# Four more half tasks of a convolution on GpSimd, paired in four phases, in a fused convolution and feed-forward kernel

## The chip, the cores and the metric

The kernel runs on one core of a Trainium2 chip. The metric is the device time of one execution in microseconds. Five engines work beside each other: TensorE (PE, with its weight loads as PEld), VectorE (DVE), ScalarE (ACT), GpSimd (POOL), and SyncE (SP), which here only issues DMAs.

## The reference

A lightweight convolution over 8 sequences of 3904 rows and 192 columns comes first: 8 heads of 24 columns, each with its own 7 causal taps (a softmax of `weight`). Its result goes through a multiplicative feed-forward network without nonlinearity.

```python
w = exp(weight - max);  w = w / (sum(w) + 1e-9)          # 8 heads x 7 taps
out[b, s, h, g] = sum_k w[h, k] * x_pad[b, s + k, h, g]   # 6 rows of zeros ahead of each sequence
x = out.reshape(31232, 192)
a = x @ w1; b = x @ w2                                    # 192 -> 1024, twice
h = a * b @ w3                                            # 1024 -> 1024
return h @ w_out                                          # 1024 -> 192
```

## The kernel before

**Tiling.** The 31232 rows are two streams (r = 0, 1) of 15616, which lie side by side on the partitions: 64 columns of each stream make 128 partitions, so 192 columns are k = 0, 1, 2. A stream is cut into rounds R = 0 to 30 of 512 rows. `first_product(R)` makes x @ w1 (pa) and x @ w2 (pb) for 8 blocks ft of 128 of the 1024 columns, each pa and pb in a pair of PSUM banks from a ring of four pairs (`banks`). ACT copies pa to `asb` (L603), DVE multiplies it with pb into `abT` (L605). `second_product(R, r)` multiplies abT with w3 @ w_out, computed once at the start, into `ops` (L621); ACT copies it to `osb` (L626) and SP sends it out.

**Phases.** Three rounds make a phase p. In its first stage the first products of its rounds run, in its second stage the second products, numbered n = 0 to 5. The order on every engine is the order in which the code issues; it is written out by hand. The first products of phase 0 run ahead of the loop, phases 1 to 8 have three rounds in both stages, phases 9 and 10 finish.

**The convolution** is done in three ways. A pair of rounds is called q: rounds 2q+1 and 2q+2.
- On TensorE: batches b of 26-row windows (`conv`, L328): x is loaded by GpSimd DMAs (`x_jobs`, L158) into `xb` tiles, a banded matrix `Aband` per head is multiplied with it, ACT copies the result to `convo` (L337). `store` (SP) writes it to the DRAM tensor `rows`, and `transposes` (SP, L426) reads it back transposed into `xT`. Batches 4, 5 and 6 (rounds 5 to 8, 13 to 16, 21 to 24) are split into units of two heads, 32 matmuls each, and `places` says after which second products of which phase a unit stands (`convolve`).
- On DVE: for the pairs in `SIDE`, `side_cast` (GpSimd DMA, L480) converts 64 columns of x to bf16 in the DRAM tensor `rows_c`, `side_transpose` (SP, L489) brings it into a `raw` tile, ACT makes the tap d = 1 (`side_first`, L494), and DVE adds the other six taps (`side_sums`, L512) into a `side` tile. A planner fills second stages with these sums by their cost (`rooms`); `starts[p]` are the tasks that begin in phase p.
- On GpSimd: seven half tasks (`BY_POOL`: a pair q, a k, one of its two rounds), one per phase in phases 2 to 8, all seven taps there (`pool_sums`): per tap a product with one tensor (L539) and an add (L559; the last, L554, writes the side tile).

`operand` gives the first product its input: the side tile for pairs in `SIDE`, xT otherwise.

**GpSimd's queue.** `points` are eight places (round, ft) in a first stage. At each, GpSimd copies two elements of abT (`pace`, L876), which makes it wait for DVE, and then issues its DMAs and the parts of its half task for that point. `clear` (L860) zeroes the rows of xb ahead of a sequence.

**SP's queue** has, at the end of a first stage, xT transposes that are due (`turn`), the raw transposes of the next phase's tasks, and `pool_transpose` (L533) for the next phase's half task; then output stores and row stores as the second products come; then what is called `late`.

Of the kernel before, what the change touches and what calls it, by code (L numbers as in the profile page):

```python
# [16 lines left out]
def kernel(  # L17
# [38 lines left out]
    def phase_of(R):  # L56
        return (R - 1) // 2

    def windows(t0, t1):
# [250 lines left out]
    def conv(b, c0, wd, evict=(nc.scalar.copy,), es=None):  # L310
        n, m, E = shape_of(b)
        es = range(E) if es is None else es
        if b not in convo_of:
            convo_of[b] = work.tile([128, n, NP, NS, Q], BF16, tag="convo", bufs=2,
                                    name="convo")
            left_of[b] = D * E
        convo = convo_of[b]
        cps = {e: banks("cps") for e in es}
        c = c0
        while c < c0 + wd:  # L320
            h = c // G
            c1 = min(h * G + G, c0 + wd)
            for j in range(4):
                xb, s = xb_of[b][j]
                for e in es:
                    for r in range(NS):
                        o = cps[e][j * C:j * C + C, r, 0:m * wd]
                        nc.tensor.matmul(  # L328
                            o.rearrange("p (w g) -> p w g", g=wd)[:, :, c - c0:c1 - c0],
                            Aband[group(r, e), h, :], xb[group(r, e), s:s + m, c:c1],  # L330
                            start=True, stop=True)
            c = c1
        for f, e in zip(evict, es):
            src = cps[e][:, :, 0:m * wd].rearrange("p r (w g) -> p r w g", g=wd)
            o = 0
            for k, lo, c in segments(c0, wd):
                f(out=convo[:, e::E, k, :, lo:lo + c]  # L337
                    .rearrange("p w r g -> p r w g"), in_=src[:, :, :, o:o + c])
                o += c
        left_of[b] -= wd * len(es)  # L340
        if not left_of[b]:
            del xb_of[b]
# [27 lines left out]
    def store(b, first=0, js=range(4)):  # L370
        n = SIZES[b] // 4
        convo = convo_of[b]
        for j in js:
            w = 0
            while w < n:
                i, m = FIRST[b] + j * n + w, 1
                t, s0, s1 = wins[i]
                while w + m < n and wins[i + m] == (t + m * ST, 0, ST):
                    m += 1
                if i < first:  # L380
                    m = first - i
                elif s1 - s0 < ST:
                    m = 1
                    if s1:
                        nc.sync.dma_start(
                            out=rows[t + s0:t + s1, :],
                            in_=convo[C * j + s0:C * j + s1, w].rearrange("s k r g -> s (k r g)"))
                else:
                    src = convo[C * j:C * j + ST, w:w + m].rearrange("s w k r g -> s w (k r g)")
                    dst = rows[t:t + ST * m, :].rearrange("(w s) c -> s w c", s=ST)  # L390
# [31 lines left out]
    def transposes(R, first=0):  # L422
        t0, t1 = max(R * CH, first), min((R + 1) * CH, TS)
        a = ring_of[R] * CH % RING + t0 - R * CH
        for k in range(NP):
            nc.sync.dma_start_transpose(  # L426
                out=xT[k][:, a:a + t1 - t0], in_=rows[t0:t1, k * 128:(k + 1) * 128])
# [21 lines left out]

    BY_POOL = ((5, 2, 0), (5, 2, 1), (8, 2, 0), (8, 2, 1), (12, 2, 0), (12, 2, 1), (13, 2, 0))  # L450
    tasks = []
# [67 lines left out]

    pool_raw, pool_acc, pool_tmp = [], [], const.tile([128, CH], FP32, name="tmp")  # L520

    def pool_tiles():
        t = stage.tile([128, 3 * CH + HALO], BF16, tag="wo", bufs=1, name="acc")
        pool_acc.append(t[:, 0:2 * CH].bitcast(FP32))
        pool_raw.append(t[:, 2 * CH:3 * CH + HALO])

# [3 lines left out]

    def pool_transpose(p, k, half):
        _, _, t0, _ = pool_half(p, k, half)
        nc.sync.dma_start_transpose(out=pool_raw[0], in_=rows_c[t0 - HALO:t0 + CH, k, :])  # L533

    def pool_sums(p, k, half):
        _, _, t0, starts = pool_half(p, k, half)

        def product(out, d):
            nc.gpsimd.tensor_scalar(  # L539
                out=out, in0=pool_raw[0][:, HALO - d:HALO - d + CH],  # L540
                scalar1=wC[:, k, K - 1 - d:K - d], scalar2=None, op0=ALU.mult)

        def job(d):
            def run():
                acc, tmp = pool_acc[0], pool_tmp
                if d == 1:
                    product(acc, 1)
                    for z in starts:
                        nc.gpsimd.memset(acc[:, z - t0:z - t0 + 1], 0.0)
                    return  # L550
                product(tmp, d)
                if d == 0:
# [8 lines left out]
            return run  # L561
        return [job(d) for d in list(range(1, K)) + [0]]

    def operand(R, k, rs):
        if phase_of(R) in side_of:
# [9 lines left out]

    abT_of = {}

# [3 lines left out]
    def first_product(R, between=None):  # L581
# [4 lines left out]
        for f0 in range(0, JT, per):  # L586
# [15 lines left out]
            asb = work.tile([128, NS, CH], BF16, tag="asb", bufs=3, name="asb")  # L602
            nc.scalar.copy(out=asb[:, :, 0:per * N], in_=pa[:, :, 0:per * N])  # L603
            if per == 1:
                nc.vector.tensor_tensor(out=ab[:, f0, :, 0:N], in0=asb[:, :, 0:N],  # L605
# [169 lines left out]
    def later_loads():  # L775
# [9 lines left out]
        for i in starts[1]:  # L785
            for f in side_cast(i):
# [22 lines left out]
             for n in [max(v for v in (2, 4) if v * shape_of(b)[1] * G <= CH)]  # L809
             for h in range(0, H, n)]  # L810
    assert sum(map(len, places.values())) == len(units)
    points = ((0, 1), (0, 4), (0, 7), (1, 2), (1, 5), (2, 0), (2, 3), (2, 6))
    jobs = {p: [] for p in range(1, len(phases))}
    for p, b, part, n in ((1, 5, 0, 0), (1, 5, 1, 4), (3, 6, 0, 0), (4, 6, 1, 0)):
# [3 lines left out]
        jobs[p + 1] += todo[n:]  # L818
    pool_from = {p: v for p, v in enumerate(BY_POOL, 1)}
    pool_sum = {p + 1: pool_sums(*v) for p, v in pool_from.items()}  # L820
    casts = [(p - 1, f) for p in starts if p > 1 for i in starts[p] for f in side_cast(i)]
    casts += [(p, f) for p, (q, k, h) in pool_from.items()
              for f in side_cast(None, (q, k, *half_of(q, h)))]
    casts.sort(key=lambda c: c[0])
    for p in jobs:
        due_now = sum(d <= p for d, _ in casts)
        ahead = max(due_now, min(len(casts), len(points) - len(jobs[p])))
        now = [f for _, f in casts[:ahead]]
        jobs[p] = now + jobs[p] if p in (1, 3) else jobs[p] + now
        del casts[:ahead]  # L830
# [32 lines left out]
    for p, (rounds, ends) in enumerate(phases):  # L863
        todo = jobs.pop(p, [])

        last = len(points) - 1
        counts = [0] * 3 + [2] * 4 if p == 1 else [2] * 2 + [1] * 5
        at = [[todo.pop(0) for _ in range(min(n, len(todo)))] for n in counts + [len(todo)]]
        if p in places:
            at[last - 1].insert(0, clear)  # L870
        for v, f in enumerate(pool_sum.pop(p, ())):
            at[v].append(f)

        def issue(R, ft, fs):
            def run():
                P(out=pace, in_=abT_of[R][0:1, ft, 1, 0:2])  # L876
                for f in fs:
                    f()
            return run

        for j, R in enumerate(rounds):
            first_product(R, {ft: issue(R, ft, at[v])
                              for v, (a, ft) in enumerate(points) if a == j and at[v]})
        assert not todo
        clear()
# [8 lines left out]
        if p in pool_from:  # L894
            pool_transpose(*pool_from[p])
# [50 lines left out]
```

## Time and profile before

| | us |
|---|---|
| median of 3 runs | 510.87 (510.76 to 511.51) |
| profiled execution | 510.92 |
| its span | 509.2 |
| DVE busy in the span | 446.4 (88%) |
| ACT busy | 347.2 (68%) |
| GpSimd busy | 229.3 (45%) |

The span is from the first to the last instruction of the program; 1.7 us of the profiled execution lie around it. A busy time is the time in which at least one instruction of that engine ran. A phase T starts here with its first pa matmul; phases 1 to 8 start at 69.93, 117.07, 166.04, 213.18, 261.24, 309.35, 356.54 and 403.73 us. In rows of a timeline, the first number is the start, the second the length, and in brackets stands the idle time of the engine ahead of it with what ended it. In rows of groups, the last parts are busy time, the mean of one in ns, and the idle time ahead.

### The profile page before, as it was taken

To read this page: it belongs to the slowest core of one execution; us is meant where nothing else is said; L and a number is where in the kernel's file an instruction comes from. 1 tells how busy PE (TensorE), PEld (TensorE's weight loads), DVE (VectorE), ACT (ScalarE), POOL (GpSimd) and SP (SyncE) were. 2 spreads that over 40 slices of the span, in tenths; PEclk is the share of its full clock that TensorE was granted. 3 is DMA by queue.
4 is the path that set the end of the run, shared out by engine and by line. 5 is a ranking of instruction groups with operands and counts; after the bars stand their busy time and mean duration, and the time that the engine had idled before them with its cause. 6 is when DMAs were issued, how large, how long until landed. Compare 5 with 4: busy or idle time off the path is not lost.

```text
span 509.2 us, 13681 instructions
## 1 busy us (share of the span) xinstructions
PE 503.8 (99%) x5758; PEld 338.5 (66%) x5758; DVE 446.4 (88%) x402; ACT 347.2 (68%) x386; POOL 229.3 (45%) x303
## 2 busy tenths in 40 slices
PE   8999999999999999999999999999999999999997
PEld 4546864595569557845875596569557855965597
DVE  7898769999999799899989999999899999999930
ACT  6786667836778776477667767763776477457752
POOL 9966101333980597079519902970573067100000
PEclk9999999999999999999999999999999999999999
DMA  9999979999955999963889337975501400230024
GB/s 136 158 162 174 173 152 177 148 163 194 159 60 159 143 158 133 229 79 23 65 219 96 24 106 127 192 110 155 102 1 43 156 4 0 84 106 1 1 63 156
DMA packets 156825, 58.45 MB, mean 115 GB/s; under 512 B 112607, under 2 KB 156763, under 8 KB 156763
## 3 DMA queue, kind: packets, MB, share of 16 engines
q0 software_dynamic: 70560, 16.85, 37.2%
q1 hardware_dynamic: 86043, 40.62, 36.1%
q8 instruction: 45, 0.74, 0.6%
q14 instruction: 17, 0.14, 0.1%
q10 hardware_dynamic: 160, 0.10, 0.1%
HBM read 33.97 MB, written 34.85 MB: 135 GB/s over the span
## 4 chain that ended last, share of the span: by engine, by line
PE 98%; DMA 1%; ACT 0%; POOL 0%; DVE 0%; issue 0%; POOLq 0%
PE ops L621 32%; PE pa L596 31%; PE pb L596 31%; PE cps L328 1%; PE wps L693 1%; DMA xb<-in_x_dram 1%; PE tps L401 0%; PE ops L646 0%; PE tps L416 0%; DVE abT L605 0%; PE cps L357 0%; ACT asb L603 0%; POOL xb L158 0%; ACT convo L337 0%; ACT osb L650 0%
## 5 line engine op out<-in xcount | busy, mean ns | idle before, releaser
L605 DVE TENSOR_TENSOR abT<-asb,pb 128x1024 bf16<-128x1024 bf16 x240 | 292.7, 1221 | 30.4 <-ACT asb L603 14.5
L603 ACT CAST asb<-pa 128x1024 bf16<-128x1024 f32 x244 | 247.0, 1012 | 64.2 <-PE pa L596 64.0
L596 PEld LDWEIGHTS <-wn 64*128 64x128 bf16 x1488 | 138.5, 94 | 79.7 <-issue 1.6
L596 PEld LDWEIGHTS <-ws 64*128 64x128 bf16 x1488 | 129.7, 94 | 70.0 <-issue 1.4
L621 PE MATMUL ops<-W_sb,abT 128*128 128x192 bf16 x1936 | 163.7, 246 | 0.0
L621 PEld LDWEIGHTS <-abT 128*128 128x128 bf16 x1936 | 158.5, 98 | 6.4 <-issue 6.4
L596 PE MATMUL pb<-xT,wn 64*128 64x512 bf16 x408 | 111.2, 376 | 0.0
L596 PE MATMUL pa<-xT,wn 64*128 64x512 bf16 x408 | 110.1, 376 | 0.1
L596 PE MATMUL pa<-xT,ws 64*128 64x512 bf16 x408 | 110.1, 376 | 0.0
L596 PE MATMUL pb<-xT,ws 64*128 64x512 bf16 x408 | 108.5, 376 | 0.0
L626 ACT COPY osb<-ops 128x768 f32<-128x768 f32 (+1 forms) x61 | 48.5, 795 | 84.7 <-PE ops L621 82.3
L876 POOL COPY pace<-abT 1x2 bf16<-1x2 bf16 x57 | 10.9, 192 | 175.5 <-DVE abT L605 155.0
L596 PE MATMUL pb<-side,wn 64*128 64x512 bf16 (+1 forms) x336 | 88.8, 368 | 0.0
L596 PE MATMUL pa<-side,ws 64*128 64x512 bf16 (+1 forms) x336 | 87.3, 369 | 0.0
L596 PE MATMUL pa<-side,wn 64*128 64x512 bf16 (+1 forms) x336 | 87.3, 369 | 0.0
L512 DVE SCALAR_TENSOR_TENSOR acc<-raw,wC,acc 128x1024 f32<-128x1024 bf16 (+2 forms) x70 | 84.6, 1209 | 2.0
L596 PE MATMUL pb<-side,ws 64*128 64x512 bf16 (+1 forms) x336 | 85.7, 368 | 0.0
L539 POOL TENSOR_SCALAR tmp<-acc,wC 128x512 f32<-128x512 bf16 x42 | 65.8, 1566 | 1.2
L559 POOL TENSOR_TENSOR acc<-acc,tmp 128x512 f32<-128x512 f32 x35 | 44.4, 1267 | 2.9
L480 POOL DMA_DIRECT2D rows_c<-in_x_dram x50 | 37.1, 744 | 4.7 <-issue 2.7
L158 POOL DMA_DIRECT2D xb<-in_x_dram x50 | 32.2, 649 | 6.9 <-DMA xb<-in_x_dram 2.2
L512 DVE SCALAR_TENSOR_TENSOR acc<-side,wC,acc 128x1024 f32<-128x1024 bf16 (+1 forms) x20 | 24.3, 1217 | 3.8 <-ACT acc L494 3.2
(76 smaller groups left out, 186.9 us busy)
## 6 DMA issues: line engine op xcount, KB each, us to landing
out_dram<-osb SPq DMA_DIRECT2D x54, 384.0 KB
xb<-in_x_dram POOLq DMA_DIRECT2D x16, 240.0 KB, 7.2
out_dram<-osb SPq DMA_DIRECT2D x12, 192.0 KB
rows_c<-in_x_dram POOLq DMA_DIRECT2D x16, 130.0 KB, 5.6
rows_c<-in_x_dram POOLq DMA_DIRECT2D x12, 128.0 KB, 5.7
rows<-convo SPq DMA_DIRECT2D x6, 240.0 KB
xb<-in_x_dram POOLq DMA_DIRECT2D x6, 228.0 KB, 4.9
w3b<-in_moe_w_dram POOLq DMA_DIRECT2D x4, 256.0 KB, 5.5
```

Source lines behind the costliest of these rows:

```text
L158: nc.gpsimd.dma_start(out=tiles[js[0]][0][group(r, e), s:s + w, :], in_=bass.AP(tensor=x.tensor, offset=(r * TS + t - PAD) * D, ap=[[D, C] ...
L328: nc.tensor.matmul(o.rearrange("p (w g) -> p w g", g=wd)[:, :, c - c0:c1 - c0], Aband[group(r, e), h, :], xb[group(r, e), s:s + m, c:c1], ...
L480: nc.gpsimd.dma_start(out=rows_c[lo:t1, k, r * Q:r * Q + Q], in_=x_rows[r * TS + lo:r * TS + t1, k * Q:k * Q + Q])
L512: nc.vector.scalar_tensor_tensor(out=side_of[p][:, k, o:o + t1 - t0] if last else a, in0=raw[:, HALO + lo - t0 - d:HALO + hi - t0 - d], sc ...
L539: nc.gpsimd.tensor_scalar(out=out, in0=pool_raw[0][:, HALO - d:HALO - d + CH], scalar1=wC[:, k, K - 1 - d:K - d], scalar2=None, op0=ALU.mult)
L559: nc.gpsimd.tensor_tensor(out=a, in0=a, in1=tmp[:, lo - t0:hi - t0], op=ALU.add)
L596: nc.tensor.matmul(p[:, r, f * N:f * N + N], w_of(i, k, r)[rs, ft * 128:(ft + 1) * 128], operand(R, k, rs), start=(k == 0), stop=(k == NP ...
L603: nc.scalar.copy(out=asb[:, :, 0:per * N], in_=pa[:, :, 0:per * N])
L605: nc.vector.tensor_tensor(out=ab[:, f0, :, 0:N], in0=asb[:, :, 0:N], in1=pb[:, :, 0:N], op=ALU.mult)
L621: nc.tensor.matmul(ops[:, g // 2, (g % 2) * D:(g % 2) * D + D], ab[:, jt, r, g * 128:(g + 1) * 128], W_sb[:, jt, :], start=(jt == 0), stop ...
L626: nc.scalar.copy(out=osb.rearrange("p (a g) d -> p a (g d)", g=2), in_=ops[:, 0:ng // 2, 0:2 * D])
L876: P(out=pace, in_=abT_of[R][0:1, ft, 1, 0:2])
```

## The change

- Four half tasks more go to GpSimd: k = 0 of the pairs 10 and 11 (`PART`), two halves each. Phases 3, 4, 5 and 6 have two half tasks (lanes 0 and 1), phases 2, 7 and 8 one as before. Their results lie in a tile taken from the `xb` ring (`part_tile`).
- Batch 6 therefore starts at the third head (`first_k`): heads 0 and 1 are not computed on TensorE, k = 0 is neither stored nor transposed. Its three units stand after n = 0, 2 and 4 of phase 5; before, its four units stood after n = 2, 4 of phase 4 and n = 1, 3 of phase 5.
- GpSimd's products have two tensors: the tap is read as a tensor of 512 equal elements.
- In a phase with two lanes ACT has made the tap d = 1 of both at the end of the phase before, after n = 4 and ahead of a unit there (`pool_first`). GpSimd does the other six taps of lane 0 and then of lane 1 at point (0, 0), behind a pace copy from asb of the first block.
- All other GpSimd work of such a phase (clear, casts, loads of x) stands at the last point (2, 6), behind the sums. The raw transposes of the next phase's tasks move to the end of the phase (`late`). The casts of half tasks from phase 4 on are due a phase earlier.
- From phase 2 on the pool transposes stand ahead of the raw transposes on SP.

```diff
+    PART = {10: (0,), 11: (0,)}
+    def beside(q, k):
+        return q in SIDE or k in PART.get(q, ())
+    def first_k(b):
+        return min(k for k in range(NP) if not beside(phase_of(tok(FIRST[b] + 1) // CH), k))
...
-            left_of[b] = D * E
+            left_of[b] = (D - first_k(b) * Q // G * G) * E
...
-                f(out=convo[:, e::E, k, :, lo:lo + c]
-                    .rearrange("p w r g -> p r w g"), in_=src[:, :, :, o:o + c])
+                if k >= first_k(b):
+                    f(out=convo[:, e::E, k, :, lo:lo + c]
+                        .rearrange("p w r g -> p r w g"), in_=src[:, :, :, o:o + c])
...
-    BY_POOL = ((5, 2, 0), (5, 2, 1), (8, 2, 0), (8, 2, 1), (12, 2, 0), (12, 2, 1), (13, 2, 0))
+    POOL_AT = {2: ((5, 2, 0),), 3: ((5, 2, 1), (10, 0, 0)), 4: ((8, 2, 0), (10, 0, 1)),
+               5: ((8, 2, 1), (11, 0, 0)), 6: ((12, 2, 0), (11, 0, 1)), 7: ((12, 2, 1),),
+               8: ((13, 2, 0),)}
+    BY_POOL = [t for ts in POOL_AT.values() for t in ts]
...
+    def pool_first(lane, p, k, half):
+        nc.scalar.activation(
+            out=pool_acc[lane], in_=pool_raw[lane][:, HALO - 1:HALO - 1 + CH],
+            func=ACT.Copy, scale=wC[:, k, K - 2:K - 1])
...
-            nc.gpsimd.tensor_scalar(
-                out=out, in0=pool_raw[0][:, HALO - d:HALO - d + CH],
-                scalar1=wC[:, k, K - 1 - d:K - d], scalar2=None, op0=ALU.mult)
+                nc.gpsimd.tensor_tensor(
+                    out=acc if d == 1 else tmp, in0=pool_raw[lane][:, HALO - d:HALO - d + CH],
+                    in1=wC[:, k, K - 1 - d:K - d].to_broadcast([128, CH]), op=ALU.mult)
...
-        return [job(d) for d in list(range(1, K)) + [0]]
+        return [job(d) for d in list(range(1 if own else 2, K)) + [0]]
...
-    places = {0: (1, 2, 3, 4), 2: (0, 1, 3, 4), 4: (2, 4), 5: (1, 3)}
+    places = {0: (1, 2, 3, 4), 2: (0, 1, 3, 4), 5: (0, 2, 4)}
...
-    casts += [(p, f) for p, (q, k, h) in pool_from.items()
+    casts += [(p if p < 3 else p - 1, f) for p, v in pool_from.items() for q, k, h in v
...
-        counts = [0] * 3 + [2] * 4 if p == 1 else [2] * 2 + [1] * 5
+        lanes = pool_sum.pop(p, ())
+        counts = [0] * 7 if len(lanes) > 1 else [0] * 3 + [2] * 4 if p == 1 else [2] * 2 + [1] * 5
...
+        elif len(lanes) > 1:
+            at[last].insert(0, clear)
+        for fs in lanes:
+            for v, f in enumerate(fs):
+                at[v if len(lanes) == 1 else 0].append(f)
+        if p == 3:
+            part_tile()
...
-                P(out=pace, in_=abT_of[R][0:1, ft, 1, 0:2])
+                P(out=pace, in_=abT_of[R][0:1, ft, 1, 0:2] if ft else asb_of[0][0:1, 1, 0:2])
...
-        late = [i for i in raws if p == 0 or i >= 5 and chain[p][0][0] <= i - 5]
+        late = [i for i in raws if p == 0 or len(lanes) > 1 or i >= 5 and chain[p][0][0] <= i - 5]
+        if p > 1:
+            for lane, t in enumerate(pool_from.get(p, ())):
+                pool_transpose(lane, *t)
...
+            if n == 4 and len(pool_from.get(p, ())) > 1:
+                for lane, t in enumerate(pool_from[p]):
+                    pool_first(lane, *t)
             if n in places.get(p, ()):
                 convolve(p)
             side_steps(p, n + 1, state)
```

More of the change, by code (lines that the diff above doesn't have):

```diff
@@ L371, in store @@
         n = SIZES[b] // 4
-        convo = convo_of[b]
+        convo = convo_of[b][:, :, first_k(b):]
+        cols = slice(first_k(b) * NS * Q, NP * NS * Q)
         for j in js:
@@ L385, in store @@
                         nc.sync.dma_start(
-                            out=rows[t + s0:t + s1, :],
+                            out=rows[t + s0:t + s1, cols],
                             in_=convo[C * j + s0:C * j + s1, w].rearrange("s k r g -> s (k r g)"))
@@ L389, in store @@
                     src = convo[C * j:C * j + ST, w:w + m].rearrange("s w k r g -> s w (k r g)")
-                    dst = rows[t:t + ST * m, :].rearrange("(w s) c -> s w c", s=ST)
+                    dst = rows[t:t + ST * m, cols].rearrange("(w s) c -> s w c", s=ST)
                     for s0, s1 in ((0, 16), (16, ST)):
@@ L425, in transposes @@
         for k in range(NP):
+            if beside(phase_of(R), k):
+                continue
             nc.sync.dma_start_transpose(
@@ L520, with part_tile @@
     pool_raw, pool_acc, pool_tmp = [], [], const.tile([128, CH], FP32, name="tmp")
+    pool_more = const.tile([128, 3 * CH + HALO], BF16, name="acc")
     def pool_tiles():
-        t = stage.tile([128, 3 * CH + HALO], BF16, tag="wo", bufs=1, name="acc")
-        pool_acc.append(t[:, 0:2 * CH].bitcast(FP32))
-        pool_raw.append(t[:, 2 * CH:3 * CH + HALO])
+        for t in (stage.tile([128, 3 * CH + HALO], BF16, tag="wo", bufs=1, name="acc"), pool_more):
+            pool_acc.append(t[:, 0:2 * CH].bitcast(FP32))
+            pool_raw.append(t[:, 2 * CH:3 * CH + HALO])
+    def part_tile():
+        t = work.tile([128, XN], BF16, tag="xb", bufs=5, name="side")
+        o = 0
+        for q, ks in PART.items():
+            n = len(ks) * 2 * CH
+            side_of[q] = t[:, o:o + n].rearrange("p (k t) -> p k t", k=len(ks))
+            o += n
     def pool_half(p, k, half):
@@ L574, in w_of @@
         return (wn if k == r else wsw)[i]
-    abT_of = {}
+    abT_of, asb_of = {}, {}
     def width(R):
@@ L603, in first_product @@
             nc.scalar.copy(out=asb[:, :, 0:per * N], in_=pa[:, :, 0:per * N])
+            asb_of[0] = asb
             if per == 1:
@@ L809 @@
              for n in [max(v for v in (2, 4) if v * shape_of(b)[1] * G <= CH)]
-             for h in range(0, H, n)]
+             for h in range(first_k(b) * Q // G, H, n)]
     assert sum(map(len, places.values())) == len(units)
@@ L828 @@
         now = [f for _, f in casts[:ahead]]
-        jobs[p] = now + jobs[p] if p in (1, 3) else jobs[p] + now
+        jobs[p] = now + jobs[p] if p in (1, 3, 4) else jobs[p] + now
         del casts[:ahead]
@@ L882 @@
             first_product(R, {ft: issue(R, ft, at[v])
-                              for v, (a, ft) in enumerate(points) if a == j and at[v]})
+                              for v, (a, ft) in enumerate(((0, 0),) + points[1:] if
+                                                          len(lanes) > 1 else points)
+                              if a == j and at[v]})
         assert not todo
-        clear()
+        if len(lanes) < 2:
+            clear()
         if p == 0:
@@ L893 @@
                 side_transpose(i)
-        if p in pool_from:
-            pool_transpose(*pool_from[p])
+        if p == 1:
+            pool_transpose(0, *pool_from[p][0])
         state = set()
```

22 lines of the change are left out of this document (9 added, 13 removed).

## The prediction

> **What bounds the kernel now.** I read the page first: TensorE is busy all the time and the chain that ended last is TensorE's.
>
> ```profile
> span 509.2 us, 13681 instructions
> PE 503.8 (99%) x5758; PEld 338.5 (66%) x5758; DVE 446.4 (88%) x402; ACT 347.2 (68%) x386; POOL 229.3 (45%) x303
> PE 98%; DMA 1%; ACT 0%; POOL 0%; DVE 0%; issue 0%; POOLq 0%
> ```
>
> A busy PE is modelled, so I then cut the span into phases (p = 2 to 5 here) at the first pa matmul of each, as the chain gives them, and read the table of windows. Columns: stretch, length, busy time of each engine.
>
> ```profile
> 117.07:166.04 48.97, 48.97 (x610) 31.77 (x612) 45.99 (x37) 38.17 (x44) 28.00 (x33) 1.00 0.80 142
> 166.04:213.18 47.14, 47.14 (x483) 31.33 (x484) 43.27 (x35) 31.15 (x32) 29.36 (x37) 1.00 1.09 165
> 213.18:261.24 48.06, 48.06 (x546) 31.52 (x548) 44.20 (x36) 34.72 (x38) 29.44 (x35) 1.00 0.63 72
> 261.24:309.35 48.11, 48.11 (x546) 32.67 (x548) 44.46 (x37) 35.69 (x39) 25.17 (x28) 1.00 0.65 113
> ```
>
> A phase without convolution takes 47.14. Four convolution units of 32 matmuls make phase 2 1.83 longer, two make phase 4 0.92 longer: 0.46 us each. So the length is matmul work; phase 5, also with two units, carries 0.05 of waiting, and that 0.05 tells how little room there is. Every phase starts with ACT copying the first pa (asb), DVE multiplying it with pb (abT), and the third pb taking the PSUM banks of the first (four pairs of banks go round). At 261.24, from the timeline (ACT, DVE, PE), the groups (the product's mean, 1221 ns) and the chain (last row):
>
> ```profile
> 262.09 1.01 ACT L603 CAST asb<-pa 128x1024 bf16<-128x1024 f32 x1
> 263.19 5.05 DVE L605 TENSOR_TENSOR abT<-asb,pb 128x1024 bf16<-128x1024 bf16 x4 [1.69 <-ACT asb L603]
> L605 DVE TENSOR_TENSOR abT<-asb,pb 128x1024 bf16<-128x1024 bf16 x240 | 292.7, 1221 | 30.4 <-ACT asb L603 14.5 <-PE cps L328 0.3
> 264.46 0.37 PE L596 MATMUL pb<-xT,wn 64*128 64x512 bf16 x1
> 264.58 0.71 PE pb L596 x6
> ```
>
> The copy starts at 262.09, the product ends at 263.19 + 1.22 = 264.41, and the third pb starts at 264.46; its piece of the chain is 0.71 instead of 0.65. A later first copy in a phase therefore costs TensorE the same time, with no more than 0.05 to spare. Behind it DVE repeats every 5.05 / 4 = 1.26 against TensorE's two pieces of 0.65 (31.1 us for the 24 pairs of a phase), so each such delay is paid once.
>
> **The change part by part.** *The removed unit.* Batch 6 loses heads 0 and 1: 12 units become 11, phase 4 has none, phase 5 has three. Sum on TensorE: -0.46 us (two units leave phase 4, one comes to phase 5). Two casts of 960 elements and two of 320 leave ACT, and four xT transposes and a third of every row store of batch 6 leave SP, all hidden work, counted as nothing.
>
> *GpSimd's sums.* Phases 3 to 6 get two half tasks each, back to back from the first copy of the phase. A half task is then six products and six adds.
>
> ```profile
> L539 POOL TENSOR_SCALAR tmp<-acc,wC 128x512 f32<-128x512 bf16 x42 | 65.8, 1566 | 1.2
> L559 POOL TENSOR_TENSOR acc<-acc,tmp 128x512 f32<-128x512 f32 x35 | 44.4, 1267 | 2.9
> 145.68 0.17 POOL L876 COPY pace<-abT 1x2 bf16<-1x2 bf16 x1
> 147.18 1.56 POOL L539 TENSOR_SCALAR tmp<-acc,wC 128x512 f32<-128x512 bf16 x1
> 148.82 1.27 POOL L554 TENSOR_TENSOR side<-acc,tmp 128x512 bf16<-128x512 f32 x1
> 150.04 1.17 POOL L876 COPY pace<-abT 1x2 bf16<-1x2 bf16 x1
> ```
>
> A two-tensor product of bf16 with a repeated tap is not in the trace. The bounds are the two-tensor add (1.27) and today's product (1.57). I take 1.27, because the add takes the same for an fp32 output (L559) and a bf16 one (148.82), and the product is that operation with another ALU function. From a product's end to its add is 0.08 today (147.18 + 1.56 to 148.82), from an add's start to what follows 1.22. So 12 x (1.35 + 1.22) = 30.8. A phase's first copy ends 1.86 after its start (262.09 + 1.01 - 261.24); with the pace copy the sums begin at about T+2.2 and end at T+33.0. In phase 4 a batch starts inside the second half task, five adds come in two pieces, an estimated 0.2 more each (a copy of two elements takes 0.17): T+34.0.
>
> That end matters because of DVE's own sums (L512, two SBUF inputs):
>
> ```profile
> 149.83 3.98 DVE L512 SCALAR_TENSOR_TENSOR acc<-raw,wC,acc 128x1024 f32<-128x1024 bf16 x3
> 198.81 5.24 DVE L512 SCALAR_TENSOR_TENSOR acc<-side,wC,acc 128x1024 f32<-128x1024 bf16 x4
> 342.17 1.28 DVE L512 SCALAR_TENSOR_TENSOR side<-side,wC,acc 128x1024 bf16<-128x1024 bf16 x1
> 215.07 5.05 DVE L605 TENSOR_TENSOR abT<-asb,pb 128x1024 bf16<-128x1024 bf16 x4 [1.91 <-ACT asb L603]
> 311.30 5.05 DVE L605 TENSOR_TENSOR abT<-asb,pb 128x1024 bf16<-128x1024 bf16 x4 [0.49 <-ACT asb L603]
> 358.49 3.76 DVE L605 TENSOR_TENSOR abT<-asb,pb 128x1024 bf16<-128x1024 bf16 x3 [0.77 <-ACT asb L603]
> ```
>
> They begin at T+32.8 (198.81 in phase 3, 342.17 in phase 6). In the only place where GpSimd meets them, at 149.83 and 150.04, the pace copy took 1.17 instead of 0.17, until L512's first instruction ended.
>
> With 1.27 the last add overlaps DVE's start by 0.2, and by 1.2 in phase 4. Before the next phase's first abT DVE idles 1.91, 1.69 (263.19), 0.49 and 0.77 after phases 3 to 6, and that covers it. Cost: nothing, but there is little left.
>
> The Trainium skill, "SBUF — State Buffer", section "SBUF: two separate sides", states that GpSimd and a DVE instruction with two SBUF inputs take a shared port pair as an exclusive lock for the whole instruction. The meeting at 149.83 agrees.
>
> *ACT's first products.* The tap d = 1 of both lanes moves to ACT, after the fifth second product (n = 4) of phases 2 to 5. What follows on ACT there:
>
> ```profile
> L494 ACT ACTIVATE acc<-raw,wC 128x512 f32<-128x512 bf16 x1 | 0.7, 724 | 0.0
> L337 ACT CAST convo<-cps 128x320 bf16<-128x320 f32 x15 | 6.6, 443 | 0.0
> L337 ACT CAST convo<-cps 128x960 bf16<-128x960 f32 x11 | 10.1, 970 | 0.0
> 162.98 0.80 ACT L626 COPY osb<-ops 128x768 f32<-128x768 f32 x1 [0.45 <-PE ops L621]
> 163.67 1.83 ACT L337 CAST convo<-cps 128x960 bf16<-128x960 f32 x2
> 166.08 0.80 ACT L626 COPY osb<-ops 128x768 f32<-128x768 f32 x1 [0.58 <-PE ops L621]
> 166.84 1.01 ACT L603 CAST asb<-pa 128x1024 bf16<-128x1024 f32 x1
> 213.21 0.80 ACT L626 COPY osb<-ops 128x768 f32<-128x768 f32 x1 [1.84 <-PE ops L621]
> 307.44 1.15 ACT L494 ACTIVATE acc<-raw,wC 128x1024 f32<-128x1024 bf16 x1
> 309.38 0.80 ACT L626 COPY osb<-ops 128x768 f32<-128x768 f32 x1 [0.79 <-PE ops L621]
> ```
>
> Two of 724 ns, overlapping by 0.1 as the casts do (two of 0.97 in 1.83), hold ACT for 1.24. From osb to the next start 0.70, the two casts 1.73, a full first product 1.15 less 0.1, osb to asb 0.76.
> - End of phases 3 and 4: nothing else stands at n = 4, ACT idles 1.84 there, 1.24 fits. Cost: nothing.
> - End of phase 2: 0.70 + 1.24 + 1.73 + 0.76 = 4.43 after the start of osb, against 166.84 - 162.98 = 3.86 today. asb is 0.57 late; less 0.05 of room: +0.5 us.
> - End of phase 5: the last unit moves to n = 4 (today n = 3), and the first product of task 11 (today at 307.44) still follows it. ACT needs 0.70 + 1.24 + 1.73 + 1.05 + 0.76 = 5.48; TensorE is ready 0.46 + 2.64 + 0.82 = 3.92 after the same point: the unit, a second product (166.08 - 162.98 less a unit), and from osb (309.38, 0.03 into its phase) to asb (262.09, 0.85 into its). asb is 1.56 late and today's room is already used: +1.55 us.
>
> For the new ACT instruction the bounds, start to start, are 0.34 (the 128x320 cast) and 1.05 (128x1024); they give 0.0 + 1.0 and 1.4 + 2.4 us for the two places. I keep 0.62: its own shape.
>
> *Queues.* In phases 3 to 6 up to 16 GpSimd DMA issues now stand behind the sums, at point (2,6), about T+33 (150.04 in phase 2). From
>
> ```profile
> L480 POOL DMA_DIRECT2D rows_c<-in_x_dram x50 | 37.1, 744 | 4.7 <-issue 2.7 <-DMA xb<-in_x_dram 1.9
> L158 POOL DMA_DIRECT2D xb<-in_x_dram x50 | 32.2, 649 | 6.9 <-DMA xb<-in_x_dram 2.2 <-issue 1.5 <-DVE w3T L682 1.0
> 46.74 0.63 POOL L158 DMA_DIRECT2D xb<-in_x_dram  x1 [0.72 <-DMA xb<-in_x_dram]
> ```
>
> 16 x 0.7 = 11.2: done by T+45, before the next phase's pace at T+49. If each waits 0.72 as at 46.74, 22 us: T+55 (a rival). SP, in phase 2: two pool transposes now stand ahead of four raw transposes, the phase's output stores, the row stores of batch 5 and twelve xT transposes, and wait for casts of point (2,6).
>
> ```profile
> 151.16 0.69 POOL L480 DMA_DIRECT2D rows_c<-in_x_dram  x1
> 154.79 1.12 SPq L533 DMA_TRANSPOSE acc<-rows_c  x1
> 180.31 17.41 SPq L426 DMA_TRANSPOSE xT<-rows  x12
> ```
>
> The old last cast landed by 154.79; two more issues of 0.7 put the second transpose at about 156.5 to 158, ready for ACT at 163.7. What is behind comes up to 4 us later; the xT transposes end at 202 instead of 197.7, their first reader is round 13 at 213.18 + 10.4. Side transposes that move to the end of phases 3 to 6 have 31 us until their first use. Output stores wait on slots that come round once a phase. All nothing; a loss would show as ACT waiting on a DMA.
>
> Sum: -0.46 + 0.5 + 1.55 = +1.6. The profiled run took 510.92 with its span of 509.2, 1.7 around it, and stands 0.05 above the median. Forecast: 510.9 + 1.6 = 512.5.
>
> **The rivals.** *ACT's lateness doesn't reach TensorE* (not slower). If the two copies' delay is taken up, because the PSUM pairs are freed in an order that leaves TensorE more than I read, only the unit is left: 510.4. For it: ACT is 68% busy, and within a phase its lateness is made up. Against: at a phase's start the third pb at 264.46 follows abT by 0.05. It decides where the slack before pb exceeds 1.5.
>
> *GpSimd's tail meets DVE's sums.* At today's 1.64 the sums take 12 x 2.86 = 34.3 and end at T+36.5, 3.7 behind DVE's start: three instructions, each making one L512 wait its turn. Less DVE's idle time after each phase 3.7 costs 1.8 + 2.0 + 1.7 (after phase 5 ACT is 1.55 late anyway) + 2.9 = 8.4 on top: 520.9. It starts to cost from a product of about 1.4, which ends at T+34.6, in phase 4 at T+35.6, 1.8 and 2.8 late: 1.1 after phase 6 and 1.1 after phase 4, 514.7. Against: the add's 1.27. The Trainium skill, "GPSIMD Engine Reference", section "Engine selection", speaks against such products: two-input operations slow, one-input ones near line rate. The trace has it the other way round, 1.57 for one tensor and 1.27 for two.
>
> *The DMA burst holds GpSimd.* Issues that wait as at 46.74 run to T+55 in phases 3 and 4; the next sums start 6 late and end at T+39, 6.2 into DVE's: (6.2 - 1.7) + (6.2 - 2.0) = 8.7 more: 521.2. Against: the waits of L480 and L158 for DMAs are 1.9 and 2.2 us over the whole span.
>
> **How the numbers follow.** Forecast 0.58, lateness absorbed 0.18, tail 0.15, burst 0.05, something that I don't see and that gains 0.04. About 0.2%, 1.0 us, is what a measurement of this kernel can tell from no change. Same: the absorbed case and 0.04 of the forecast, its lower price for ACT's instruction (511.5): 0.22. Slower: the rest of the forecast, tail and burst: 0.74. Faster 0.04: TensorE has no more than the unit to lose. The range reaches from just under the absorbed case, 510.2, to 514.5, which takes in ACT's upper price (510.9 - 0.46 + 3.8 = 514.2) and a product of nearly 1.4; the tail beyond that (0.11), the burst and the unseen gain are left out.
>
> **What would show it.** The phase from 309 on begins with asb late and a pb piece some 1.5 long behind abT; the phase after 166 one 0.5 long; phase 4 takes 47.1; phase 5 48.5; GpSimd's products read about 1.27; L512 keeps 1285. Wrong if L512 or its wait on GpSimd grows, if ACT's small first products wait on a DMA, or if the phases from 166 and 308 on start without a gap.

## The result

The changed kernel takes 513.17 us, the median of 6 runs (512.60 to 514.44), against 510.81 for the kernel before: a ratio of 1.0046, 95% interval 1.0034 to 1.0059. In a second session it took 513.03 against 510.96, 1.0044 (1.0030 to 1.0057). The forecast was 512.5, with a range of 510.2 to 514.5.

The profiled run is the slowest of the six, 514.44 with a span of 512.7: TensorE's granted clock was 0.5 from 9.0 to 12.4 us, so that every phase begins 1.7 us late. Below, lengths of phases are compared, and a second profile of the same kernel without this (run a1 below, 512.92, span 511.1) is used where the total matters. The page of the changed kernel, the lines that answer to the three shown of before:

```profile
span 512.7 us, 13669 instructions
PE 505.9 (99%) x5726; PEld 337.2 (66%) x5726; DVE 445.9 (87%) x402; ACT 349.2 (68%) x390; POOL 256.0 (50%) x340
PE 95%; ACT 2%; DMA 1%; issue 1%; DVE 1%; POOL 0%; ACTq 0%; DVEq 0%; POOLq 0%
```

TensorE has 32 matmuls fewer, GpSimd 27 us more work, and ACT, which was at 0% of the chain that ended last, is now in it with 2%. The table of windows, phases 2 to 6 of the changed kernel, columns as in the prediction (stretch, length, busy time of PE, PEld, DVE, ACT and POOL; then the granted clock, the DMA share and GB/s):

```profile
118.81:167.79 48.98, 48.98 (x610) 31.72 (x612) 45.92 (x37) 38.71 (x46) 27.40 (x39) 1.00 0.95 144
167.79:215.40 47.61, 47.30 (x482) 32.39 (x484) 43.08 (x35) 32.77 (x35) 38.32 (x42) 1.00 0.94 144
215.40:262.54 47.14, 47.14 (x482) 31.14 (x484) 43.28 (x36) 32.37 (x34) 39.48 (x49) 1.00 0.79 107
262.54:311.07 48.53, 48.53 (x578) 31.64 (x580) 45.64 (x37) 36.50 (x42) 34.17 (x36) 1.00 0.82 119
311.07:359.65 48.58, 47.64 (x482) 32.36 (x484) 44.38 (x37) 31.53 (x33) 33.32 (x34) 1.00 0.69 114
```

Phase 4 lost its two units (48.06 to 47.14), phase 5 got one more (48.11 to 48.53). Phase 3 (47.14 before) is 0.47 longer and phase 6 (356.54 - 309.35 = 47.19 before) 1.39 longer, and in both TensorE is not busy for part of it: 47.30 and 47.64. What ended these waits stands in the chain of waits of the changed kernel, at the end of phase 5 and the start of phase 6:

```profile
307.99 0.02 ACT osb L652
...
308.69 1.34 ACT acc L559 x2
310.02 1.71 ACT convo L345 x2
311.73 0.14 ACT acc L508
...
312.66 0.50 ACT osb L652
...
313.34 1.05 ACT asb L628
...
314.41 1.23 DVE abT L631
...
315.69 0.82 PE pb L621 x6
```

This is the order on ACT that the prediction wrote down: osb, the two new first products (L559), the casts of the unit (L345), the full first product of a task (L508), osb, asb, and behind asb DVE's product and TensorE's third pb.

From the first pa matmul of phase 2 to that of TensorE's last block (rounds 28 to 30, where a matmul is 64x256) TensorE takes 371.79 us in both profiles of the changed kernel and 370.49 before: 1.30 more. The rest of the cost lies behind that point. The timelines of PE, the first matmul of the last block, of before and then of the second profile of the changed kernel (span 511.1):

```profile
487.49 0.28 PE L596 MATMUL pa<-side,wn 64*128 64x256 bf16 x1
```

```profile
488.78 0.28 PE L621 MATMUL pa<-side,wn 64*128 64x256 bf16 x1
```

To the end of the span are 509.2 - 487.49 = 21.7 before and 511.1 - 488.78 = 22.3 now: 0.6 more, in a stretch that the change does not touch. Together the two parts are the 1.9 us between the spans.

### The profile page after: what moved, and what is told of

Read it like the earlier page. It is cut to its first block, busy times and chain, and to the rows that moved or that the text cites. A ratio compares the mean times of both kernels' runs of the same rounds, so it can differ in the third digit from the quotient of the medians.

```text
span 512.7 us, 13669 instructions
## 1 busy us (share of the span) xinstructions
PE 505.9 (99%) x5726; PEld 337.2 (66%) x5726; DVE 445.9 (87%) x402; ACT 349.2 (68%) x390; POOL 256.0 (50%) x340
## 4 chain that ended last, share of the span: by engine, by line
PE 95%; ACT 2%; DMA 1%; issue 1%; DVE 1%; POOL 0%; ACTq 0%; DVEq 0%; POOLq 0%
PE ops L647 31%; PE pa L621 31%; PE pb L621 30%; PE wps L719 1%; PE cps L335 1%; DMA xb<-in_x_dram 1%; DVE abT L631 1%; ACT convo L345 1%; ACT asb L628 1%; ACT acc L559 1%; PE tps L410 0%; PE ops L672 0%; PE tps L425 0%; PE cps L365 0%; POOL xb L165 0%
## 5 line engine op out<-in xcount | busy, mean ns | idle before, releaser
L621 PE MATMUL pa<-xT,ws 64*128 64x512 bf16 x376 | 104.4, 380 | 0.0
L621 PE MATMUL pb<-xT,wn 64*128 64x512 bf16 x376 | 104.2, 378 | 0.0
L621 PE MATMUL pa<-xT,wn 64*128 64x512 bf16 x376 | 103.9, 380 | 0.1
L621 PE MATMUL pb<-side,wn 64*128 64x512 bf16 (+1 forms) x368 | 101.0, 369 | 1.2 <-DVE abT L631 0.7
L621 PE MATMUL pa<-side,wn 64*128 64x512 bf16 (+1 forms) x368 | 99.3, 369 | 0.1
L621 PE MATMUL pa<-side,ws 64*128 64x512 bf16 (+1 forms) x368 | 99.4, 369 | 0.0
L621 PE MATMUL pb<-side,ws 64*128 64x512 bf16 (+1 forms) x368 | 97.6, 369 | 0.0
L526 DVE SCALAR_TENSOR_TENSOR acc<-raw,wC,acc 128x1024 f32<-128x1024 bf16 (+2 forms) x70 | 84.6, 1208 | 4.1 <-ACT acc L508 2.0
L584 POOL TENSOR_TENSOR acc<-acc,tmp 128x512 f32<-128x512 f32 (+6 forms) x60 | 70.4, 1176 | 4.3
L572 POOL TENSOR_TENSOR tmp<-acc,wC 128x512 f32<-128x512 bf16 x66 | 68.5, 1038 | 3.5
L908 POOL COPY pace<-abT 1x2 bf16<-1x2 bf16 x28 | 4.9, 174 | 110.9 <-DVE abT L631 110.7
L526 DVE SCALAR_TENSOR_TENSOR acc<-side,wC,acc 128x1024 f32<-128x1024 bf16 (+1 forms) x20 | 24.3, 1217 | 3.7 <-ACT acc L508 3.2
```

Source lines behind the costliest of these rows:

```text
L526: nc.vector.scalar_tensor_tensor(out=side_of[p][:, k, o:o + t1 - t0] if last else a, in0=raw[:, HALO + lo - t0 - d:HALO + hi - t0 - d], sc ...
L572: nc.gpsimd.tensor_tensor(out=acc if d == 1 else tmp, in0=pool_raw[lane][:, HALO - d:HALO - d + CH], in1=wC[:, k, K - 1 - d:K - d].to_broa ...
L584: nc.gpsimd.tensor_tensor(out=a, in0=a, in1=tmp[:, lo - t0:hi - t0], op=ALU.add)
L621: nc.tensor.matmul(p[:, r, f * N:f * N + N], w_of(i, k, r)[rs, ft * 128:(ft + 1) * 128], operand(R, k, rs), start=(k == 0), stop=(k == NP ...
```

## The experiments

**My theory:** ACT's lateness at the starts of phases 3 and 6 is the cost, less the saved unit. **Rivals:** ACT's lateness is absorbed and something else costs; GpSimd's tail collides with DVE's sums; the two-tensor products cost by themselves. Every ratio is against the kernel before, run in the same session. The labels a1 to d2 are those that the expectations use. "Body" is the stretch from phase 2's first matmul to the last block's, "tail" from there to the end of the span, both from the profile of the run; before they are 370.49 and 21.7.

**The change again** (a1), unaltered.

> The changed kernel once more, on the chip of the next three. By the theory (ACT's late copies, +0.5 and +1.4, less one unit of 0.46) 512.2 to 512.4; its median stood at 513.2, so some 0.8 more is not accounted for: it should show here again if it is the program's own, and shrink if it came with the runs (a slow clock in the first 13 us of the profiled execution).

Measured: 513.03, 1.0044 (1.0030 to 1.0057); body 371.79, tail 22.3.

**First products one second product earlier in phase 5** (a2).

```diff
-            if n == 4 and len(pool_from.get(p, ())) > 1:
+            if n == (3 if p == 5 else 4) and len(pool_from.get(p, ())) > 1:
```

> ACT's two first products of phase 5 stand after n = 3, where ACT idles 1.84 us, instead of n = 4. Theory of ACT's late copy: the stall at the start of phase 6 goes, 1.35 us less than the changed kernel, phases 5 and 6 together 95.8 instead of 97.1 us, no pb piece of 0.82 behind abT there; that of phase 3 stays. Rival, that GpSimd's load or the transfers behind it hold TensorE: no change to the changed kernel, 0.0.

Measured: 511.99, 1.0022 (1.0010 to 1.0033), 1.04 below the run beside it; body 370.59, so 1.20 of the 1.39 in phase 6 is gone. Nothing but the place of two ACT instructions was changed.

**The same in phase 2 too** (a3; n == 2 there).

```diff
+            if n == {2: 2, 5: 3}.get(p, 4) and len(pool_from.get(p, ())) > 1:
```

> The same, and in phase 2 the two first products stand after n = 2, where ACT idles 1.36. Theory: both stalls gone, 1.8 us less than the changed kernel, and 0.46 (the removed unit) below the kernel before: 510.4. If transposes haven't landed by then (they were issued from 153.4 to 156.2 and ACT wants them at 160.1), ACT waits and some of the 0.5 comes back. Rival, load on GpSimd or transfers: it stays with the changed kernel, 2 us above before.

Measured: 511.12, 1.0006 (0.9997 to 1.0014), 1.9 below the change: body 370.11, 0.38 below the kernel before. The time did not follow below before, since the tail is 22.3.

**The products alone** (a4), in the kernel before.

```diff
-            nc.gpsimd.tensor_scalar(
+            nc.gpsimd.tensor_tensor(
...
-                scalar1=wC[:, k, K - 1 - d:K - d], scalar2=None, op0=ALU.mult)
+                in1=wC[:, k, K - 1 - d:K - d].to_broadcast([128, CH]), op=ALU.mult)
```

> The kernel before with the two-tensor products alone; seven half tasks, all placed as before. Theory: GpSimd is hidden in the first stages, products of 1.04 instead of 1.57 change nothing, 510.8 within 0.3; GpSimd busy 26 us less (49 products of 0.53). Rival, that two-tensor products take the port from DVE: L605 and L512 longer than 1.22 and 1.285, and a slower kernel.

Measured: 511.22, 1.0002 (0.9994 to 1.0011), body 370.49, tail 21.7: the products by themselves neither cost nor gain. Groups of this kernel, POOL, shapes kept apart:

```profile
L539 POOL TENSOR_TENSOR tmp<-acc,wC 128x512 f32<-128x512 bf16 x42 | 43.9, 1044 | 0.5
```

**The first products made twice** (b1), so that ACT has 1.24 us more in front of phases 3 to 6.

```diff
                     pool_first(lane, *t)
+                    pool_first(lane, *t)
```

> The changed kernel with each of ACT's small first products issued twice (the second writes the same values). 1.24 us more on ACT after n = 4 of phases 2 to 5. Theory of ACT's late copy: 1.24 more at the starts of phases 3 and 6, and at the starts of phases 4 and 5, where one pair fitted under 1.84 us of idle time, 0.70 + 2.48 + 0.76 = 3.94 against 2.64 + 0.82 = 3.46, so 0.4 each: +3.3 us over the changed kernel, 516.3. Rival, that ACT's time is absorbed and GpSimd or the transfers hold TensorE: +0.

Measured: 517.18, 1.0120 (1.0106 to 1.0134); body 376.17, 4.4 more than the change, where 3.3 was expected. The pieces of pb behind abT are 0.82 long at all four starts (171.06, 218.87, 266.68, 318.16), where the change has two of them. The 1.1 beyond the expectation is the price of the doubled pair: the second product of a lane writes the same tile, and on ACT it starts some 0.75 behind the first instead of 0.62 (starts at the end of phase 2: 163.53, 164.29, 164.92, 165.66), so the four hold ACT for 2.75 instead of 2.48, 0.27 more at each of four places. With the two runs above this settles the first rival: ACT's work at that place reaches TensorE, both ways.

**One-tensor products in the change** (b2), as the kernel before has them.

```diff
-                nc.gpsimd.tensor_tensor(
+                nc.gpsimd.tensor_scalar(
...
-                    in1=wC[:, k, K - 1 - d:K - d].to_broadcast([128, CH]), op=ALU.mult)
+                    scalar1=wC[:, k, K - 1 - d:K - d], scalar2=None, op0=ALU.mult)
```

> The changed kernel with the one-tensor products of before (1.57 instead of 1.04). Theory of the tail: the sums of phases 3 to 6 end at T+36.5, 3.7 behind the start of DVE's own sums; L512's group gets longer, and DVE reaches the next abT late: +8 us by the prediction's sum, 521. Rival, that the two engines share without loss (GpSimd alone waits): 513, L512's counterpart stays at 1285.

Measured: 535.16, 1.0483 (1.0439 to 1.0526): 24 above the kernel before where 10 was expected, so some 22 above the change instead of 8. The mechanism of the tail rival is real, and I had priced it far too low. The timeline of POOL, end of the sums of phase 4:

```profile
248.34 1.40 POOL L584 TENSOR_TENSOR acc<-acc,tmp 128x448 f32<-128x448 f32 x2
249.84 1.56 POOL L572 TENSOR_SCALAR tmp<-acc,wC 128x512 f32<-128x512 bf16 x1
251.48 2.38 POOL L584 TENSOR_TENSOR acc<-acc,tmp 128x448 f32<-128x448 f32 x2
253.97 2.41 POOL L572 TENSOR_SCALAR tmp<-acc,wC 128x512 f32<-128x512 bf16 x1
...
262.72 1.18 POOL L908 COPY pace<-abT 1x2 bf16<-1x2 bf16 x1
...
264.45 5.89 POOL L494 DMA_DIRECT2D rows_c<-in_x_dram  x8
```

and its groups on DVE, shapes kept apart:

```profile
L526 DVE SCALAR_TENSOR_TENSOR acc<-raw,wC,acc 128x1024 f32<-128x1024 bf16 x55 | 76.7, 1394 | 1.6
L526 DVE SCALAR_TENSOR_TENSOR side<-raw,wC,acc 128x1024 bf16<-128x1024 bf16 x11 | 15.8, 1439 | 0.3
```

Where the two meet, GpSimd's product takes 2.41 instead of 1.56 and its pair of adds 2.38 instead of 1.40, and DVE's sums grow to 1394 and 1439 on average, from 1284 for both in the change. The Trainium skill, "SBUF — State Buffer", section "SBUF: two separate sides", has a port pair locked for the whole instruction of GpSimd or of a DVE instruction with two SBUF inputs, while the other waits; these rows agree. The chain of waits shows what I had left out:

```profile
205.44 1.18 POOL pace L908
206.61 3.60 POOL rows_c L494 x5
210.21 9.34 DMA rows_c<-in_x_dram
...
266.04 9.65 DMA rows_c<-in_x_dram
...
283.65 1.46 PE pa L621 x6
285.12 1.28 PE pb L621 x6
```

The DMA issues stand behind the late sums, the chain then waits 9 us for their transfers, and the next phase's sums and raw data wait with it. The sums of phase 4 begin at 222.36, 8.8 us into the phase, where the change has 2.1. So the tail rival sets off the rival of the DMA burst, and the lateness of phase 3 comes back in phase 4 and, larger, in phase 5: phases 3 to 7 last 47.6, 52.8, 62.2, 48.8 and 48.6 us, against 47.6, 47.1, 48.5, 48.6 and 47.1 in the change. I had charged each phase once.

Some of this is TensorE's clock. In this profile the granted clock was 0.5 from 224.5 to 227.9 and from 279.1 to 289.3 us, during or just behind waits of TensorE of 3.2 and 8.7 us, and pieces there take 1.28 instead of 0.65. TensorE worked for 8.9 us of these stretches, so an estimated 4.4 us at most went that way. The other 16 to 17 of the 20.9 us between the two spans are still twice the 8 expected.

**The tail.** The last TensorE instruction comes at the same distance from the last block in both kernels (18.7); what is later are the last output issues on SP. The timelines of SP, before:

```profile
504.85 0.46 SPq L635 DMA_DIRECT2D out_dram<-osb  x1
...
505.97 0.41 SPq L652 DMA_DIRECT2D out_dram<-osb  x1
506.59 0.33 SPq L652 DMA_DIRECT2D out_dram<-osb  x1
```

and the change, second profile (span 511.1):

```profile
506.15 1.20 SPq L661 DMA_DIRECT2D out_dram<-osb  x1
507.44 0.45 SPq L661 DMA_DIRECT2D out_dram<-osb  x1
507.97 0.40 SPq L678 DMA_DIRECT2D out_dram<-osb  x1
508.47 0.40 SPq L678 DMA_DIRECT2D out_dram<-osb  x1
```

One issue takes 1.20 instead of 0.46, and the three behind it queue up on SP; the last starts 19.7 into the last block instead of 19.1. In the records of DMA packets, a packet of 16 KB on the queue "instruction" (45 in a run) starts at 505.9 there. In before the nearest one is at 502.0, and the issue at 502.2 takes 1.25, where SP has time to spare. Two ideas on what moves it: SP's own stream of instructions, or TensorE's, which has 64 fewer (32 matmuls and 32 weight loads).

**SP's stream shifted** (b3) by four small stores at the end of phase 7, in the kernel with both first products earlier.

```diff
+        if p == 7:
+            for d in pad_d:
+                nc.sync.dma_start(out=d, in_=taps)
```

> As a3 (ACT's first products earlier in phases 2 and 5), with four small extra DMAs on SP's queue at the end of phase 7, where it is idle. In the changed kernel and in a1 to a3 one output issue 2 us before the end takes 1.1 to 1.3 instead of 0.46 while a packet of the instruction queue runs, and the last two issues come 0.6 late; in the kernel before the same long issue lies at 502.2 and is covered. Theory: it is bound to a place in SP's instruction stream, so four more instructions ahead of it move it away from the end: 0.6 below a3, 510.5. Rival, that it belongs to the end of the program or to DMA load there: 511.1 and the same long issue.

Measured: 511.99, 1.0011 (1.0002 to 1.0020); the long issue (1.07) stays, and so does the packet's place, 17.2 us into the last block (17.1 in a3). SP's stream it is not.

**The last unit earlier** (b4), on top of that.

```diff
-    places = {0: (1, 2, 3, 4), 2: (0, 1, 3, 4), 5: (0, 2, 4)}
+    places = {0: (1, 2, 3, 4), 2: (0, 1, 3, 4), 5: (0, 2, 3)}
```

> As b3, and the last unit of phase 5 after n = 3 instead of n = 4, as before the change: at n = 4 only the first product of task 11 stands. Theory: a3 still shows a pb piece of 0.82 after 308, ACT being 0.70 + 1.73 + 1.05 + 0.76 = 4.24 behind n = 4 against 3.92; that 0.2 goes too: 510.3, 0.5 below the kernel before. Rival: as b3.

Measured: 511.46, 1.0006 (0.9997 to 1.0015). Body 369.86: 0.63 less than before, and phases 3, 4 and 6 take 47.1 each; tail 22.5. This is the unit's saving, eaten by the tail, which is 0.8 longer.

**TensorE's count of instructions put back** to that of before, by shorter and more warm-up matmuls; once with the starts mended (c1), once in the change alone (c2).

```diff
-    warm(6)
+    warm(3, small=35)
```

> As b4 without the extra DMAs, and 35 matmuls of 16 columns in the place of three of 512 at the very start, where TensorE only warms up: TensorE's instruction count is again that of the kernel before (11518 instead of 11454). b3 kept the long issue in its place, so it doesn't hang on SP's stream. New theory: the packets of the instruction queue, 16384 bytes each, are TensorE's (45 of 256 instructions are 11520); 64 instructions fewer move each fetch 64 instructions later, from 502.0 to 504.5, onto the issue of the last output but two. With the old count the packet is back near 502, the last issues come 0.6 earlier: 510.3, 0.5 below the kernel before. Rival, that the packet belongs to something else at the end: 511.4 as b4.

> The changed kernel with that instruction count alone. Theory: 0.6 less than the changed kernel, 512.4; the starts of phases 3 and 6 stay late. Rival: 513.0.

Measured: 511.80, 1.0026 (1.0013 to 1.0040), and 514.03, 1.0059 (1.0047 to 1.0071). Neither time came out as expected. The tail did: 21.7 in both, the packet is back at 502.2 and 504.1 (14.6 and 14.5 us into the last block), with the long issue beside it and covered (timeline of SP, the second of the two, the last block at 489.7):

```profile
504.38 1.12 SPq L663 DMA_DIRECT2D out_dram<-osb  x1
...
508.75 0.33 SPq L680 DMA_DIRECT2D out_dram<-osb  x1
```

What was won there was lost ahead of phase 2, which begins 0.8 to 0.9 later than in before and in the change: in phase 0 TensorE now waits within a product, for nothing that the profile shows (chain of the same kernel):

```profile
48.01 0.32 PE pa L623
48.33 0.63 issue
48.97 0.80 PE pa L623 x5
```

Instruction packets lie near it (46.4 and 46.5), but that they cause it is not shown: before has one at 47.0 and d1 one at 46.6, without such a wait. Nor is this the whole of it. The profiled executions (511.05 and 513.08) are the fastest of their kernels, 0.7 and 1.0 below the medians, and what the others lost is not on record.

**One output transfer instead of two** for the second sub-round of round 29, so that nothing is issued where the packet begins; once with the starts and the unit mended (d1), once in the change alone (d2).

```diff
-        n = ng if R < NR - 4 else ng // 2
+        n = ng if R < NR - 4 or (R, r) == (NR - 2, NS - 1) else ng // 2
```

> The changed kernel with ScalarE's first products two and one products earlier in phases 2 and 5, the unit that ends last in phase 5 earlier too (as in the fourth run of the second group, whose median was 511.46 where the kernel before had 511.15), and one edit at the end: the output of round 29's second sub-round goes out in one transfer instead of two, so that no SP issue begins where TensorE's instruction packet runs, 504.3 to 504.7 us into the span. Nothing at the start is touched. Theory (the last 0.6 us of the change's cost is one SP issue of 1.05 to 1.30 us instead of 0.46 during that packet): from TensorE's last block to the end 21.6 instead of 22.2, and 0.6 below the same kernel without the edit: 510.4 to 510.8, some 0.5 below the kernel before. Rival (the packet lengthens whichever issue comes next, or the larger transfer ends later): the tail stays at 22.2 and the time at 511.1 to 511.5.

> The changed kernel with that one output edit and nothing else. The same theory: 0.6 below the changed kernel's 513.0, so 512.4, with phases 3 and 6 beginning as late as in the changed kernel. The rival: 513.0, the tail at 22.2.

Measured: 510.89 against 510.91, 0.9998 (0.9989 to 1.0007), and 512.69, 1.0033 (1.0022 to 1.0043). The rival held: the tails are 22.3 in both. The merged issue goes through in 0.37, and the next one takes the 1.01 (timeline of SP, the second kernel):

```profile
506.51 0.37 SPq L661 DMA_DIRECT2D out_dram<-osb  x1
507.51 1.01 SPq L661 DMA_DIRECT2D out_dram<-osb  x1
508.62 0.41 SPq L678 DMA_DIRECT2D out_dram<-osb  x1
509.11 0.39 SPq L678 DMA_DIRECT2D out_dram<-osb  x1
```

Measured from the kernel before of their own session, both medians lie 0.3 lower than in the kernels without this edit (b4 and a1), within overlapping intervals; with the tails unchanged I don't ascribe that to it. The first of the two is the best form of the change found here, and it is level with the kernel before; no version is shown to be faster.

## Why the prediction was right, and where it wasn't

- **The removed unit, -0.46: right.** Phase 4 lost 0.92 and phase 5 gained 0.42; with all waits mended the body is 0.63 shorter.
- **ACT's first products, +0.5 and +1.55: right in place, mechanism and nearly in size,** +0.47 and +1.39. In the chain, asb stands 5.35 behind osb (307.99 to 313.34), where the prediction had 5.48 for the same five steps. Moving and doubling the first products confirmed it. One of the signs that I named was not the right one: I had looked for pieces of pb 1.5 and 0.5 long, and both are 0.82. The wait stands ahead of the piece: in phase 6 the third pb starts 4.62 after the first pa (315.69 - 311.07), where phase 5 of before has 3.22 (264.46 - 261.24).
- **The products: the bounds were wrong.** I took 1.27 between 1.27 and 1.57, and it is 1.04, below both. Groups of the changed kernel on POOL and DVE, shapes kept apart:

```profile
L572 POOL TENSOR_TENSOR tmp<-acc,wC 128x512 f32<-128x512 bf16 x66 | 68.5, 1038 | 3.5
L584 POOL TENSOR_TENSOR acc<-acc,tmp 128x512 f32<-128x512 f32 x50 | 63.3, 1267 | 3.9
```

```profile
L526 DVE SCALAR_TENSOR_TENSOR acc<-raw,wC,acc 128x1024 f32<-128x1024 bf16 x55 | 70.6, 1284 | 3.6 <-ACT acc L508 2.0
```

  The two-tensor add that I took for its price reads fp32, the product reads bf16; that this is the reason was not tested. L526 keeps 1284, so the tail rival did not occur: the sums of phase 4 end at 247.65, half a microsecond before DVE's begin (timelines of POOL and of DVE):

```profile
246.38 1.27 POOL L579 TENSOR_TENSOR side<-acc,tmp 128x512 bf16<-128x512 f32 x1
```

```profile
248.16 1.28 DVE L526 SCALAR_TENSOR_TENSOR side<-raw,wC,acc 128x1024 bf16<-128x1024 bf16 x1
```

  With my 1.27 the sums would have ended 2.8 later (12 x 0.23), 2.2 into DVE's, and not the 1.2 of the prediction: from an add's start to the next product are 1.34 here, not the 1.22 that I had read where a pace copy followed. That DVE's idle time would have covered this was argued, and the run with one-tensor products speaks against such a reckoning. "Costs nothing, but there is little left" came out right by luck, because the price was wrong to the good side.
- **The tail rival's price, 8.4: too low by a factor of two and a half** (some 22 above the change, of which an estimated 4.4 at most are TensorE's clock), since the lateness is carried into the next phase by the DMA issues behind the sums.
- **The queues, nothing: right, with less room than I gave.** I had the burst done 4 us ahead of the next pace. It ends 1.1 us ahead of it (timeline of POOL, changed kernel, end of phase 4; in brackets the waits for earlier transfers):

```profile
257.20 1.24 POOL L494 DMA_DIRECT2D rows_c<-in_x_dram  x2 [2.99 <-DMA rows_c<-in_x_dram]
...
262.88 0.53 POOL L165 DMA_DIRECT2D xb<-in_x_dram  x1 [1.19 <-DMA rows_c<-in_x_dram]
264.53 0.17 POOL L908 COPY pace<-asb 1x2 bf16<-1x2 bf16 x1 [1.12 <-ACT asb L628]
```

- **The sum, +1.6: short of the +2.1 to +2.4 measured.** Up to TensorE's last block it is 1.3, so the sum was 0.3 too high there, most of it in ACT's two terms. The missing term is the tail's 0.6: output issues at the end of the program, which I had counted as untouched. The 0.2 to 0.5 beyond these 1.9 lie between profiled executions and medians and stay open; the fastest runs of the two kernels are 1.9 to 2.0 apart (512.52 against 510.65, 512.60 against 510.64). At the end of the program the long issue goes with the instruction packet, as the two runs with the merged transfer show, and the packet's place with TensorE's count of instructions: in the ten profiles with 64 fewer the last packet begins 17.06 to 17.25 us into the last block, in the four with the count of before 14.46 to 14.66. That mending it gains time was not shown, as no run did so without a loss elsewhere.

## What to carry to other kernels

Before you put work on an engine "that is only 68% busy", write down its instructions in order around the next hand-over that the bounding engine waits for: 1.24 us cost 1.4 at one such place, 0.47 at another and nothing at two, and the same instructions one or two places earlier in the order cost next to nothing. Price a collision of two engines with everything that is queued behind the late one, and ask whether the lateness comes back next time round. When a change removes instructions, look at the last microseconds too: what ends the program can shift without having been touched.

## What the runs showed of the hardware

- GpSimd, 128x512, bf16 in and fp32 out: a product of a tensor with a repeated column of another takes 1038 to 1044 ns, a product with one scalar per partition 1566 (1627 on average in b2, where some of them meet DVE's sums), and an add of two fp32 tensors 1267. The Trainium skill, "GPSIMD Engine Reference", section "Engine selection", calls one-input operations roughly line-rate and two-input ones about twice as slow as on VectorE; of the three forms measured here, the one-input one is the slowest.
- From 2 us ahead of the last block to the end, an output issue on SP takes 0.33 to 0.48 us, and 1.0 to 1.6 when it begins while a 16 KB packet of the instruction queue is under way (all 24 such issues of the 14 profiles). Earlier in the program this does not hold: 17 of 26 issues that begin during such a packet take 0.37, and others are as long without one (2.0 at 69 and 71 us in a1), so a packet alone does not make an issue long.
- There are 45 such packets in a run of some 11,500 TensorE instructions, about 256 to a packet. The records don't name the engine that they serve; with 64 TensorE instructions fewer the last one came 17.1 instead of 14.6 us into the last block, with the count put back 14.5 and 14.6.
